# One gated mix of two attentions on one core: the phi of the segment tiles moved by a tile, its memory sums joined in pairs, weight loads and gates through GpSimd's queue

## The chip, the core and the metric

The kernel runs on one core of a Trainium2 chip. Five engines work in it, each through its own queue and strictly in the order in which the kernel was written: TensorE (PE, matrix products; PEld is its weight load), VectorE (DVE), ScalarE (ACT), GpSimd (POOL) and SyncE (SP), which here only starts DMA transfers. An engine that must wait for a semaphore holds up all that is queued behind the waiting instruction. The metric is device microseconds of one execution, smaller is better. The kernel before takes 1767.47 us, the median of three runs from 1766.33 to 1767.89 us.

## The reference, cut to what matters

```
x: [2048, 512]; 32 heads of 16
g = sigmoid(sum(x * gate_w))                        # per row
a = softmax(q k^T / 4) v @ A_wo                     # side A: plain attention, q k v = x @ wqkv
# side B: q, k, v = x @ wq, x @ wk, x @ wv, cut in 4 segments of 512 rows
phi(t) = t + 1 where t > 0, else exp(t)
g_h = sigmoid(beta)                                 # per head
M, z = 0, 0
for s in range(4):
    a_dot = causal softmax attention inside segment s
    a_mem = (phi(q_s) @ M) / (phi(q_s) @ z + 1e-6)
    o_s   = g_h * a_mem + (1 - g_h) * a_dot
    M += phi(k_s)^T @ v_s ;  z += sum over rows of phi(k_s)
b = o @ B_wo
out = g * a + (1 - g) * b
```

All is float32. phi is computed as max(t, 0) + exp(min(t, 0)).

## The kernel before, in words

**Two stages.** The first makes all projections and the memory M, z of side B; the second, from `wide` and `score_part` on, runs the attention itself, 32 units of side A and 32 of side B, and the output products. The change is all in the first stage.

**Slots.** The first stage is a row of slots. One slot is one projection tile: `slot()` (L350 to L363) issues twelve matmuls of 128x128 by 128x512 (L361), each factor split into a rounded value and its rest. After every third matmul comes a *place* (0 to 3) in which functions run that were posted for this slot with `post` (from here on) or `post_at` (a fixed slot). The list of a place runs in the order of posting. So the order of work on every engine is written out by hand, tile by tile.

**Side A first, then the segments.** Side A has 40 slots (chunks of 512 rows; the q tiles of the last two chunks are made later). Then come four segments of side B with twelve slots each: four q tiles (one per *octet* of eight heads), four v tiles, four k tiles. Below, slots are counted from the first segment's first q tile: segment c has q in 12c to 12c+3, v in 12c+4 to 12c+7, k in 12c+8 to 12c+11.

**What follows a q or k tile** is in `qk_tile` (L406). One slot after the matmuls run, in place 0, `e0`: ScalarE copies PSUM to `full` (L427), rounds it to `q1` (L428), SP stores that, and for tiles that need phi GpSimd takes `mn` = min(full, 0) (L432). In place 1, `e1`: VectorE makes the rest `q2` (L435), SP stores it, ScalarE takes `ex` = exp(mn) (L439). In place 2, `e2`: VectorE adds max(full, 0) to it (L444, `ph`). phi is needed for the k tiles of segments 0 to 2 and the q tiles of segments 1 to 3. `mn` and `ex` have one buffer each; `jk` of the gate (L525, VectorE) shares `mn`'s buffer.

**The memory.** For a k tile `mem_k` transposes phi on TensorE (L596, `tps`) at place 3 of the slot after the one in which `e2` ran, and ScalarE copies the result (`pt`, L598). After the second tile of a pair of octets `mem_k2` multiplies both by v (L610, `mps`, 64 small matmuls without the transposes), and `mem_k3` (L615) adds the sums to `mrun`, weighs them by the head's gate and a block mask into `mbd`, and spreads z into `zbd`: three small VectorE instructions for each octet, six for the pair (L618 or L620, L621, L622). `mem_q` (L564) reads all of it in slots 18, 30 and 42: `num` (L569, 32 matmuls) and `den` (L573) on TensorE.

**Maxima of the attention to come** are woven in. `some_max` runs at place 3 of slots 12 to 17 and 19 of a segment's round (and of all slots from 36 on but 42): four products (L236, `sm`) into four PSUM buffers, each read by one VectorE maximum (L269, `pm`). The next four products need these buffers back, and so does `num`. In segment 3, `load_gate` puts `jk` into slots 40 and 41.

**Weights and chunks** are loaded by `halves` (L375): two DMAs of 512 KB into `raw` tiles of which there are three, then a split by ScalarE (L397) and VectorE (L398) a few slots later. The three weights of the segments are loaded in this way during the last eight slots of side A, on SP's queue, where the stores of tiles are too (L424 for q and k, L470 for v). A load whose `raw` buffer is still being split waits at the head of its queue.

**Gates of the heads.** `betas` (L512) spreads 32 values of beta over the partitions with a matmul (L518) in slot 20 of side A, and takes the sigmoid.

Of the kernel before, what the change touches and what calls it, by code (L numbers as in the profile page):

```python
# [10 lines left out]
F32 = mybir.dt.float32  # L11
F32R = mybir.dt.float32r
AF = mybir.ActivationFunctionType
ALU = mybir.AluOpType
# [5 lines left out]
D = 512  # L20
# [27 lines left out]
def gated_mix(ctx, tc, x, xT, wqkv, a_wo, b_wq, b_wk, b_wv, b_wo, beta, gate_w, out):  # L48
# [278 lines left out]
    with ExitStack() as p0:  # L327
# [23 lines left out]
        def post(slots, place, f):  # L351
            posted.setdefault((now[0] + slots, place), []).append(f)
# [21 lines left out]

        def halves(pool, tag, src, load_slot, split_slot, tiles=None):  # L375

            hold = {}

            def load(i):
                t = tiles[i] if tiles else None  # L380
                if t is None:
                    t = raws.tile([128, 2, D], F32, tag="raw", name="raw")
                if isinstance(t, list):
                    for k in range(2):
                        nc.sync.dma_start(t[k], src[256 * i + 128 * k:256 * i + 128 * k + 128])
                        hold["raw", 2 * i + k] = t[k]
                else:
                    nc.sync.dma_start(t, src[256 * i:256 * i + 256].rearrange("(k p) d -> p k d", p=128))
                    for k in range(2):
                        hold["raw", 2 * i + k] = t[:, k]  # L390
# [21 lines left out]
        def qk_tile(side, w, xc, o, dst, then=None, ps=None, n0=0):  # L412
# [28 lines left out]
            def e2():  # L441
                if then:
                    ph["ph"] = wk.tile([128, CH], F32, tag="ph", name="ph", bufs=4)
                    nc.vector.scalar_tensor_tensor(ph["ph"], full, 0.0, ph["ex"], op0=ALU.max, op1=ALU.add)  # L444
                    then(ph["ph"])
            for place, f in enumerate((e0, e1, e2)):
                post(n0, place, f)

# [58 lines left out]
        gw = wk1.tile([128, D], F32, tag="gw", name="gw")  # L507
        beta8 = wk1.tile([8, NO], F32, name="beta8")
        post_at(8, 0, lambda: nc.gpsimd.dma_start(beta8, beta.rearrange("(o h) -> h o", h=8)))
        post_at(16, 0, lambda: nc.gpsimd.dma_start(gw, gate_w.unsqueeze(0).broadcast_to([128, D])))  # L510

        def betas():  # L512

            ps = me_ps.tile([128, CH], F32, tag="me", name="bt")
            spread = wk1.tile([8, 128], F32, name="spread")
            one8 = identf[0:8, 0:8]
            nc.vector.tensor_copy(spread.rearrange("p (h q) -> p h q", q=16), one8.unsqueeze(2).broadcast_to([8, 8, 16]))
            nc.tensor.matmul(ps[:, 0:NO], spread, beta8, start=True, stop=True)  # L518
            nc.scalar.activation(gh, ps[:, 0:NO], AF.Sigmoid)
            nc.vector.tensor_scalar(ogh, gh, -1.0, 1.0, op0=ALU.mult, op1=ALU.add)  # L520
        post_at(20, 2, betas)

        def gate_logit(xg, b, col):
            jk = wk1.tile([128, D], F32, tag="mn", name="jk")
            nc.vector.scalar_tensor_tensor(jk, xg[:, b], 1.0, gw, op0=ALU.mult, op1=ALU.mult,  # L525
                                           accum_out=glog[:, col:col + 1])
# [10 lines left out]
        for c in range(NCH):  # L537
            s0 = now[0] - (4 if c in LATER else 0)
            xn = halves(xp, "x", xchunk((c + 1) % NCH), s0 + (3 if c == 0 else 4), s0 + 8)
            if c == NCH - 1:  # L540
                wBq = halves(wp, "wq", b_wq, s0 + 7, s0 + 10)
                wBv = halves(wp, "wk", b_wv, s0 + 9, s0 + 13)
                wBk = halves(wp, "wv", b_wk, s0 + 11, s0 + 15)
            if c == 0:
                first_tiles(wAq, xc)
            for o in range(NO if 0 < c and c not in LATER else 0):
                qk_tile("A", wAq, xc, o, qd["A", o, c])
            for o in range(NO):
                qk_tile("A", wAk, xc, o, kd["A", o, c])
            v_tiles("A", wAv, xc, c)  # L550
            xc = xn

        mrun = [st.tile([128, 2, 17], F32, name=f"mrun{o}") for o in range(NO)]
        mbd = [st.tile([128, 2, DH], F32, name=f"mbd{o}") for o in range(NO)]
        zbd = st.tile([128, NO, 32], F32, name="zbd")
# [8 lines left out]
        def mem_q(c):  # L564

            banks = [me_sm.tile([128, CH], F32, tag="sm", name="num") for _ in range(4)]
            for o in range(NO):
                for i in range(4):
                    nc.tensor.matmul(banks[i][32 * o:32 * o + 32], mbd[o][32 * i:32 * i + 32].rearrange("p h e -> p (h e)"),  # L569
                                     pqs[o][32 * i:32 * i + 32], start=True, stop=True, tile_position=(32 * i, 32 * o))  # L570
# [34 lines left out]
        def mem_k2(both, c, vs):  # L605
            mps = me_ps.tile([128, 2, 2, 17], F32, tag="me", name="mps")
            for n, (o, pt) in enumerate(both):
                for b in range(4):
                    for i in range(4):
                        nc.tensor.matmul(mps[32 * i:32 * i + 32, n].rearrange("p h e -> p (h e)"), pt[:, b, 32 * i:32 * i + 32],  # L610
                                         vs[:, 2 * o + i // 2, b, 2 * (i % 2):2 * (i % 2) + 2].rearrange("p h e -> p (h e)"),
                                         start=(b == 0), stop=(b == 3), tile_position=(0, 32 * i))
            post(1, 0, lambda: mem_k3([o for o, _ in both], c, mps))

        def mem_k3(os, c, mps):  # L615
            for n, o in enumerate(os):
                if c == 0:
                    nc.vector.tensor_copy(mrun[o], mps[:, n])  # L618
                else:
                    nc.vector.tensor_add(mrun[o], mps[:, n], mrun[o])  # L620
                nc.vector.scalar_tensor_tensor(mbd[o], mrun[o][:, :, 0:16], gh[:, o:o + 1], bmask, op0=ALU.mult, op1=ALU.mult)  # L621
                nc.vector.tensor_scalar_mul(zbd[:, o, 0:8], heads8, mrun[o][:, 0, 16:17])  # L622

# [550 lines left out]
```

## Time and profile before

| | |
|---|---|
| median of three runs | 1767.47 us |
| the profiled execution's own time | 1768.02 us |
| its span in the trace | 1766.3 us |
| busy in the span: PE, DVE, ACT, POOL | 99%, 88%, 81%, 36% |
| first projection matmul (L455) | 5.91 us |
| `num` of segments 1, 2, 3 starts | 182.27, 230.20, 281.01 us |
| first scores of the second stage (L810) | 300.61 us |

Times in the trace count from the start of the span. A row of the timeline has the start, the length, engine, line, operation, output and inputs, and how many instructions are merged; in brackets stands the idle time of the engine ahead of it with what ended it. Instructions of one engine overlap at their ends, so what one costs in a dense row is the distance from its start to the next one's start. A row of the chain of waits has start, length, engine or queue, and line. A row of the windows has, for a stretch, each engine's busy time, then the granted TensorE clock (1.00 is full), the share of the DMA engines and GB/s.

### The profile page before, as it was taken

How to read it: one execution, taken by the hardware profiler on the slowest of the kernel's cores; microseconds unless marked ns; L12 is line 12 of the kernel's file. 1: busy time of each engine (PE TensorE's matmuls, PEld its weight loads, DVE VectorE, ACT ScalarE, POOL GpSimd, SP SyncE). 2: the span in 40 equal slices, each digit the busy share in tenths (PEclk: the TensorE clock that was granted, in tenths of full speed). 3: DMA queues.
4: the chain of work that ended last, by engine and by line, in shares of the span. 5: the costliest groups of instructions: out<-in, count | busy, mean ns of one | idle time of the engine just before them, and what ended most of it. 6: DMA issues, size and time to landing. Idle time of an engine off the chain costs nothing.

```text
span 1766.3 us, 41299 instructions
## 1 busy us (share of the span) xinstructions
PE 1755.0 (99%) x15231; PEld 901.0 (51%) x15231; DVE 1559.8 (88%) x3330; ACT 1435.2 (81%) x2751; POOL 642.5 (36%) x749
## 2 busy tenths in 40 slices
PE   9999999999999999999999999999999999999999
PEld 8886666544444444444444444444444444444444
DVE  4236667999999999999999999999999999999931
ACT  5454444888888898888888888888888888888884
POOL 3002222415161416443434343344434253434343
PEclk9999999999999999999999999999999999999999
DMA  7667665434453536554444545444545444544542
GB/s 244 219 227 224 201 219 185 124 111 135 125 157 108 148 109 177 147 142 134 132 141 123 147 128 147 129 145 110 155 115 151 127 137 120 151 120 143 150 154 62
DMA packets 149657, 261.60 MB, mean 148 GB/s; under 512 B 38568, under 2 KB 61128, under 8 KB 148944
## 3 DMA queue, kind: packets, MB, share of 16 engines
q1 hardware_dynamic: 148096, 257.56, 49.4%
q8 instruction: 121, 1.98, 0.5%
q0 software_dynamic: 1216, 1.14, 0.3%
q14 instruction: 80, 0.66, 0.1%
q10 hardware_dynamic: 144, 0.26, 0.1%
HBM read 174.39 MB, written 83.25 MB: 146 GB/s over the span
## 4 chain that ended last, share of the span: by engine, by line
PE 92%; DVE 3%; ACT 1%; POOL 1%; DMA 1%; issue 1%; SPq 0%; POOLq 0%; DVEq 0%; ACTq 0%
PE ops L155 40%; PE st L810 27%; PE sm L236 13%; PE pr L361 8%; PE sm L155 2%; DVE pm L269 2%; POOL mn L432 1%; DVE ph L444 1%; PE pr L455 1%; DMA qdB<-q 0%; DVE q L435 0%; DVE jk L525 0%; PE mt_ps L226 0%; ACT ex L439 0%; DMA raw<-xT 0%
## 5 line engine op out<-in xcount | busy, mean ns | idle before, releaser
L833 ACT ACTIVATE p<-st 128x512 f32<-128x512 f32 x2261 | 1190.7, 601 | 147.6 <-PE sm L236 92.1
L269 DVE TENSOR_REDUCE pm<-sm 128x1 f32<-128x512 f32 x2048 | 1276.7, 680 | 7.0 <-PE sm L236 7.0
L236 PE MATMUL sm<-kA,qA 48*128 48x512 f32 x2048 | 670.3, 425 | 3.8 <-DVE pm L269 2.1
L810 PE MATMUL st<-qA,kA 50*128 50x512 f32 x2014 | 656.0, 431 | 0.0
L155 PE MATMUL ops<-p,vA 128*17 128x256 f32 (+3 forms) x6360 | 552.6, 445 | 0.6 <-DMA qB<-mt 0.6
L810 PEld LDWEIGHTS st<-qA,kA 50*128 50x128 f32 x2014 | 326.8, 185 | 423.0 <-ACT p L833 382.7
L236 PEld LDWEIGHTS sm<-kA,qA 48*128 48x128 f32 x2048 | 340.5, 185 | 21.4 <-DVE pm L269 13.9
L934 POOL TENSOR_TENSOR rcp<-rec,minus 128x32 f32<-128x32 f32 x43 | 234.2, 5447 | 84.2 <-DMA rec<-dend 76.3
L284 DVE CUSTOM_DVE_ANT_0 rest<-sm,mask 128x128 f32<-128x128 f32 (+3 forms) x512 | 245.1, 479 | 0.7 <-PE sm L236 0.7
L155 PEld LDWEIGHTS ops<-p,vA 128*17 128x17 f32 x6360 | 129.3, 96 | 213.4 <-issue 182.3
L814 POOL TENSOR_SCALAR_AFFINE_SELECT p<-p 128x512 f32<-128x512 f32 x128 | 79.4, 636 | 289.9 <-ACT p L833 285.4
L236 PE MATMUL sm<-kB,qB 48*128 48x128 f32 (+3 forms) x512 | 166.0, 384 | 0.0
L810 PE MATMUL st<-qB,kB 50*128 50x512 f32 (+1 forms) x495 | 105.3, 329 | 0.3 <-ACT mt L229 0.3
L435 DVE TENSOR_TENSOR q<-full,q 128x512 fp32r<-128x512 f32 x56 | 38.6, 688 | 72.8 <-ACT q L428 66.3
L810 PEld LDWEIGHTS st<-qB,kB 50*128 50x128 f32 x495 | 68.5, 186 | 62.2 <-ACT p L833 50.5
L155 PE MATMUL ops<-p,vB 128*17 128x128 f32 (+3 forms) x1504 | 88.3, 350 | 0.0
L236 PEld LDWEIGHTS sm<-kB,qB 48*128 48x128 f32 x512 | 80.0, 184 | 0.0
L217 POOL CAST ms<-nm 128x16 fp32r<-128x16 f32 x32 | 6.3, 197 | 193.6 <-DVE nm L213 191.6
L432 POOL TENSOR_SCALAR mn<-full 128x512 f32<-128x512 f32 x24 | 37.8, 1576 | 96.9 <-ACT full L427 76.5
L427 ACT COPY full<-pr 128x512 f32<-128x512 f32 x56 | 32.7, 584 | 40.6 <-PE pr L361 34.5
L217 POOL CAST ms<-pm 128x16 fp32r<-128x16 f32 x32 | 6.3, 197 | 127.0 <-DVE pm L284 127.0
L950 POOL TENSOR_TENSOR v<-v,inv 128x512 f32<-128x512 f32 x31 | 39.8, 1285 | 27.4 <-DMA inv<-rdA 23.8
(197 smaller groups left out, 1578.9 us busy)
## 6 DMA issues: line engine op xcount, KB each, us to landing
kA<-kdA SPq DMA_DIRECT2D x256, 128.0 KB
vA<-vdA SPq DMA_DIRECT2D x31, 544.0 KB
kA<-kdA SPq DMA_DIRECT2D x256, 64.0 KB
qB<-qdB SPq DMA_DIRECT2D x192, 64.0 KB
kB<-kdB SPq DMA_DIRECT2D x192, 64.0 KB
kdA<-q SPq DMA_DIRECT2D x32, 256.0 KB
qdB<-q SPq DMA_DIRECT2D x32, 256.0 KB
qA<-qdA SPq DMA_DIRECT2D x64, 128.0 KB
```

Source lines behind the costliest of these rows:

```text
L155: behind[0] = nc.tensor.matmul(*args, **kw)
L236: nc.tensor.matmul(ps[:, n0:n0 + n], rows(qt[u][:, :, s * 128:(s + 1) * 128], h, 48), rows(k[:, :, k0:k0 + n], h, 48), start=True, stop=True)
L269: nc.vector.tensor_reduce(pm[:, h, s, kc:kc + 1], ps, axis=AX.X, op=ALU.max)
L284: nc.vector.tensor_tensor_reduce(out=tri["rest"][:, 0:w], in0=ps[:, n0:n0 + w], in1=tri["mask"][:, CH - w:], scale=-1.0, scalar=3.0e38, op ...
L361: nc.tensor.matmul(ps, l(a, k), r(b, k), start=(n == 0), stop=(n == 11))
L432: nc.gpsimd.tensor_scalar_min(ph["mn"], full, 0.0)
L435: nc.vector.tensor_sub(q2, full, q1.bitcast(F32))
L810: nc.tensor.matmul(ps[:, n0:n0 + CH - q0], rows(k[:, :, b * 128:(b + 1) * 128], h, 50), rows(q[:, :, q0:], h, 50), start=True, stop=True)
L814: nc.gpsimd.affine_select(out=x, in_=x, pattern=[[0, 4], [1, 128]], base=0, channel_multiplier=-1, compare_op=ALU.is_ge, fill=0.0)
L833: nc.scalar.activation(p[:, h], ps, AF.Exp, scale=SCALE)
L934: eng.tensor_tensor(r, rec, minus, op=ALU.pow)
L950: eng.tensor_mul(k["v"], k["v"], k["inv"])
```

## The change

Five edits:

1. **phi later.** `e2` is posted one slot later and in place 1 (it was place 2 of the slot of `e0` and `e1`). It runs there ahead of the next tile's `e1`. All that hangs on it (transposes, memory sums) moves by one slot; `mem_q` stays where it was.
2. **Memory sums for two octets at once.** `mrun` and `mbd` hold a pair of octets; `mem_k3` has three VectorE instructions for the pair. The gate and the block mask are multiplied ahead of time into `gmask`, in `betas`.
3. **Segment weights** are loaded from GpSimd's queue (three weights, two DMAs each).
4. **Gates of the heads** are spread by eight DMAs on GpSimd's queue in slot 8 of side A, straight into `gh`; the matmul, its operand and its PSUM tile are gone. `betas` has four more VectorE instructions.
5. **`jk`** uses the buffer of `dn` (`keep_den`) and not that of `mn`.

```diff
@@ -372,7 +372,7 @@
                 post_at(6 + i, 1 + 2 * r, lambda t=t, r=r: nc.gpsimd.dma_start(
                     raw(t)[64 * r + 48:64 * r + 50], ones.unsqueeze(1).broadcast_to([2, 2, CH])))
 
-        def halves(pool, tag, src, load_slot, split_slot, tiles=None):
+        def halves(pool, tag, src, load_slot, split_slot, tiles=None, queue=nc.sync):
 
             hold = {}
 
@@ -382,10 +382,10 @@
                     t = raws.tile([128, 2, D], F32, tag="raw", name="raw")
                 if isinstance(t, list):
                     for k in range(2):
-                        nc.sync.dma_start(t[k], src[256 * i + 128 * k:256 * i + 128 * k + 128])
+                        queue.dma_start(t[k], src[256 * i + 128 * k:256 * i + 128 * k + 128])
                         hold["raw", 2 * i + k] = t[k]
                 else:
-                    nc.sync.dma_start(t, src[256 * i:256 * i + 256].rearrange("(k p) d -> p k d", p=128))
+                    queue.dma_start(t, src[256 * i:256 * i + 256].rearrange("(k p) d -> p k d", p=128))
                     for k in range(2):
                         hold["raw", 2 * i + k] = t[:, k]
 
@@ -443,8 +443,9 @@
                     ph["ph"] = wk.tile([128, CH], F32, tag="ph", name="ph", bufs=4)
                     nc.vector.scalar_tensor_tensor(ph["ph"], full, 0.0, ph["ex"], op0=ALU.max, op1=ALU.add)
                     then(ph["ph"])
-            for place, f in enumerate((e0, e1, e2)):
-                post(n0, place, f)
+            post(n0, 0, e0)
+            post(n0, 1, e1)
+            post(n0 + 1, 1, e2)
 
         def first_tiles(w, xc):
 
@@ -505,23 +506,21 @@
         wAk = halves(wp, "wk", wqkv[:, D:2 * D], None, 2, [None, pairs[0]])
         wAv = halves(wp, "wv", wqkv[:, 2 * D:3 * D], 1, 4, [early[1].rearrange("p (k d) -> p k d", k=2), pairs[1]])
         gw = wk1.tile([128, D], F32, tag="gw", name="gw")
-        beta8 = wk1.tile([8, NO], F32, name="beta8")
-        post_at(8, 0, lambda: nc.gpsimd.dma_start(beta8, beta.rearrange("(o h) -> h o", h=8)))
+        gmask = wk1.tile([128, NO, 2, DH], F32, name="gmask")
+        for h in range(8):
+            post_at(8, 0, lambda h=h: nc.gpsimd.dma_start(gh[DH * h:DH * h + DH], beta.rearrange("(o h) -> h o", h=8)[h:h + 1]
+                                                          .broadcast_to([DH, NO])))
         post_at(16, 0, lambda: nc.gpsimd.dma_start(gw, gate_w.unsqueeze(0).broadcast_to([128, D])))
 
         def betas():
-
-            ps = me_ps.tile([128, CH], F32, tag="me", name="bt")
-            spread = wk1.tile([8, 128], F32, name="spread")
-            one8 = identf[0:8, 0:8]
-            nc.vector.tensor_copy(spread.rearrange("p (h q) -> p h q", q=16), one8.unsqueeze(2).broadcast_to([8, 8, 16]))
-            nc.tensor.matmul(ps[:, 0:NO], spread, beta8, start=True, stop=True)
-            nc.scalar.activation(gh, ps[:, 0:NO], AF.Sigmoid)
+            nc.scalar.activation(gh, gh, AF.Sigmoid)
             nc.vector.tensor_scalar(ogh, gh, -1.0, 1.0, op0=ALU.mult, op1=ALU.add)
+            for o in range(NO):
+                nc.vector.tensor_scalar_mul(gmask[:, o], bmask, gh[:, o:o + 1])
         post_at(20, 2, betas)
 
         def gate_logit(xg, b, col):
-            jk = wk1.tile([128, D], F32, tag="mn", name="jk")
+            jk = wk1.tile([128, D], F32, tag="dn", name="jk")
             nc.vector.scalar_tensor_tensor(jk, xg[:, b], 1.0, gw, op0=ALU.mult, op1=ALU.mult,
                                            accum_out=glog[:, col:col + 1])
 
@@ -538,9 +537,9 @@
             s0 = now[0] - (4 if c in LATER else 0)
             xn = halves(xp, "x", xchunk((c + 1) % NCH), s0 + (3 if c == 0 else 4), s0 + 8)
             if c == NCH - 1:
-                wBq = halves(wp, "wq", b_wq, s0 + 7, s0 + 10)
-                wBv = halves(wp, "wk", b_wv, s0 + 9, s0 + 13)
-                wBk = halves(wp, "wv", b_wk, s0 + 11, s0 + 15)
+                wBq = halves(wp, "wq", b_wq, s0 + 7, s0 + 10, queue=nc.gpsimd)
+                wBv = halves(wp, "wk", b_wv, s0 + 9, s0 + 13, queue=nc.gpsimd)
+                wBk = halves(wp, "wv", b_wk, s0 + 11, s0 + 15, queue=nc.gpsimd)
             if c == 0:
                 first_tiles(wAq, xc)
             for o in range(NO if 0 < c and c not in LATER else 0):
@@ -550,8 +549,8 @@
             v_tiles("A", wAv, xc, c)
             xc = xn
 
-        mrun = [st.tile([128, 2, 17], F32, name=f"mrun{o}") for o in range(NO)]
-        mbd = [st.tile([128, 2, DH], F32, name=f"mbd{o}") for o in range(NO)]
+        mrun = [st.tile([128, 2, 2, 17], F32, name=f"mrun{i}") for i in range(2)]
+        mbd = [st.tile([128, 2, 2, DH], F32, name=f"mbd{i}") for i in range(2)]
         zbd = st.tile([128, NO, 32], F32, name="zbd")
         nc.gpsimd.memset(zbd, 0.0)
 
@@ -566,7 +565,7 @@
             banks = [me_sm.tile([128, CH], F32, tag="sm", name="num") for _ in range(4)]
             for o in range(NO):
                 for i in range(4):
-                    nc.tensor.matmul(banks[i][32 * o:32 * o + 32], mbd[o][32 * i:32 * i + 32].rearrange("p h e -> p (h e)"),
+                    nc.tensor.matmul(banks[i][32 * o:32 * o + 32], mbd[o // 2][32 * i:32 * i + 32, o % 2].rearrange("p h e -> p (h e)"),
                                      pqs[o][32 * i:32 * i + 32], start=True, stop=True, tile_position=(32 * i, 32 * o))
             dps = me_ps.tile([128, CH], F32, tag="me", name="den")
             for o in range(NO):
@@ -610,16 +609,16 @@
                         nc.tensor.matmul(mps[32 * i:32 * i + 32, n].rearrange("p h e -> p (h e)"), pt[:, b, 32 * i:32 * i + 32],
                                          vs[:, 2 * o + i // 2, b, 2 * (i % 2):2 * (i % 2) + 2].rearrange("p h e -> p (h e)"),
                                          start=(b == 0), stop=(b == 3), tile_position=(0, 32 * i))
-            post(1, 0, lambda: mem_k3([o for o, _ in both], c, mps))
-
-        def mem_k3(os, c, mps):
-            for n, o in enumerate(os):
-                if c == 0:
-                    nc.vector.tensor_copy(mrun[o], mps[:, n])
-                else:
-                    nc.vector.tensor_add(mrun[o], mps[:, n], mrun[o])
-                nc.vector.scalar_tensor_tensor(mbd[o], mrun[o][:, :, 0:16], gh[:, o:o + 1], bmask, op0=ALU.mult, op1=ALU.mult)
-                nc.vector.tensor_scalar_mul(zbd[:, o, 0:8], heads8, mrun[o][:, 0, 16:17])
+            post(1, 0, lambda: mem_k3(both[0][0] // 2, c, mps))
+
+        def mem_k3(i, c, mps):
+            if c == 0:
+                nc.vector.tensor_copy(mrun[i], mps)
+            else:
+                nc.vector.tensor_add(mrun[i], mps, mrun[i])
+            nc.vector.tensor_mul(mbd[i], mrun[i][:, :, :, 0:DH], gmask[:, 2 * i:2 * i + 2])
+            nc.vector.tensor_mul(zbd[:, 2 * i:2 * i + 2, 0:8], heads8.unsqueeze(1).broadcast_to([128, 2, 8]),
+                                 mrun[i][:, :, 0, DH:DH + 1].broadcast_to([128, 2, 8]))
 
 
         def some_max():
```

## The prediction

> **What bounds the kernel now.** First the page.
>
> ```profile
> span 1766.3 us, 41299 instructions
> PE 1755.0 (99%) x15231; PEld 901.0 (51%) x15231; DVE 1559.8 (88%) x3330; ACT 1435.2 (81%) x2751; POOL 642.5 (36%) x749
> ...
> PE 92%; DVE 3%; ACT 1%; POOL 1%; DMA 1%; issue 1%; SPq 0%; POOLq 0%; DVEq 0%; ACTq 0%
> ```
>
> TensorE is the bound: 92% of the chain that ended last. No edit takes away TensorE work but one small matmul, so the change can win only where TensorE waits in the first stage: the 3% of DVE, and part of the ACT, POOL and DMA shares of the chain. A busy PE of 99% hides such waits, since the end of a matmul is modelled. So I read starts in TensorE's timeline. An undisturbed stretch comes first, then the rounds of the three segments.
>
> ```profile
> 293.38 0.73 PE L236 MATMUL sm<-kA,qA 48*128 48x512 f32 x4
> ...
> 296.99 0.73 PE L236 MATMUL sm<-kA,qA 48*128 48x512 f32 x4
> ```
>
> One slot with four max products lasts 296.99 - 293.38 = 3.61 us.
>
> ```profile
> 154.51 0.73 PE L236 MATMUL sm<-kA,qA 48*128 48x512 f32 x4
> 155.18 0.77 PE L610 MATMUL mps<-vs,pt 128*32 128x34 f32 x64
> 155.88 0.65 PE L596 MATMUL tps<-identf,ph 128*128 128x128 f32 x4
> 156.29 0.49 PE L361 MATMUL pr<-xh,wql 128*128 128x512 f32 x1
> ...
> 160.16 2.29 PE L236 MATMUL sm<-kA,qA 48*128 48x512 f32 x4 [0.84 <-DVE pm L269]
> ...
> 165.70 1.39 PE L236 MATMUL sm<-kA,qA 48*128 48x512 f32 x4
> ...
> 182.27 0.71 PE L569 MATMUL num<-ph,mbd 32*32 32x512 f32 x16
> ...
> 202.76 0.73 PE L236 MATMUL sm<-kA,qA 48*128 48x512 f32 x4
> ...
> 230.20 0.71 PE L569 MATMUL num<-ph,mbd 32*32 32x512 f32 x16
> ...
> 250.69 0.73 PE L236 MATMUL sm<-kA,qA 48*128 48x512 f32 x4
> ...
> 272.53 0.41 PE L226 MATMUL mt_ps<-identf,ms 128*32 128x128 f32 x2
> ...
> 281.01 1.14 PE L569 MATMUL num<-ph,mbd 32*32 32x512 f32 x32
> ```
>
> By distances of starts, `mps` costs 0.70 us and `tps` 0.41. From `sm` of the round's first slot (12) to `num` (slot 18) stand six slots, two `mps` and two `tps`: 6 x 3.61 + 2 x 0.70 + 2 x 0.41 = **23.88 us**, were nothing waited for. Found are 182.27 - 154.51 = 27.76, 230.20 - 202.76 = 27.44, and 281.01 - 250.69 = 30.32, of which `mt_ps` has a right to about 0.34. The excess is 3.88 + 3.56 + 6.10 = **13.54 us**. It sits where the reader sees `sm` of 2.29 and 1.39 us where 0.73 is normal: products that wait for maxima (L269) to give their PSUM back. In the third round there is more:
>
> ```profile
> 273.00:277.00 4.00, 4.00 (x11) 3.17 (x12) 3.96 (x9) 0.71 (x2) 0.00 (x0) 0.57 0.32 110
> ```
>
> The granted clock is 0.57 for these 4 us, right behind such a wait: 0.43 x 4 = 1.7 of the 6.10 us.
>
> Why are the maxima late? VectorE, GpSimd and ScalarE in the second round:
>
> ```profile
> 206.81 0.69 DVE L444 SCALAR_TENSOR_TENSOR ph<-full,ex 128x512 f32<-128x512 f32 x1 [2.04 <-ACT ex L439]
> 207.42 2.48 DVE L269 TENSOR_REDUCE pm<-sm 128x1 f32<-128x512 f32 x4
> 209.81 0.18 DVE L620 TENSOR_TENSOR mrun<-mps,mrun 128x34 f32<-128x34 f32 x1
> ...
> 210.85 0.69 DVE L435 TENSOR_TENSOR q<-full,q 128x512 fp32r<-128x512 f32 x1
> 211.46 0.68 DVE L444 SCALAR_TENSOR_TENSOR ph<-full,ex 128x512 f32<-128x512 f32 x1
> ```
>
> ```profile
> 204.35 1.77 POOL L432 TENSOR_SCALAR mn<-full 128x512 f32<-128x512 f32 x1 [3.40 <-DVE jk L525]
> ```
>
> ```profile
> 206.15 0.63 ACT L439 ACTIVATE ex<-mn 128x512 f32<-128x512 f32 x1 [2.92 <-POOL mn L432]
> ```
>
> `ph` stands ahead of the maxima in VectorE's queue and idles it for 2.04 us, waiting for `ex`, which waits for `mn`, which waited for `jk`, whose buffer it shares. So VectorE is late by waiting, not by work.
>
> **The change, part by part.** *phi later (edit 1) and `jk` apart (edit 5).* `ex` gets a whole slot more, and `mn` no longer waits for `jk`. What is late next? VectorE's own work. By starts: four maxima 209.81 - 207.42 = 2.39, the six small ones 210.85 - 209.81 = 1.04, `q2` 0.61, `ph` 207.42 - 206.81 = 0.61. Maxima begin about 0.54 after `sm`:
>
> ```profile
> 297.53 2.48 DVE L269 TENSOR_REDUCE pm<-sm 128x1 f32<-128x512 f32 x4 [0.38 <-PE sm L236]
> ```
>
> In the new order VectorE has, from one group of maxima to the next, 2.39 + `ph` 0.61 + `q2` 0.61 = 3.61 us, in slots 14 and 16 `mem_k3` besides, and in slot 17 no `q2`. TensorE's distances between the `sm` groups become 4.02 (slot 12, one `tps`), 4.72 (13, `mps` and `tps`), 4.02, 4.31, 3.61, 3.61. With `mem_k3` at half, 0.52, VectorE needs 3.61, 4.13, 3.61, 4.13, 3.00, and then 0.54 + 2.39 = 2.93 up to `num`. Each is below its distance; the least margin is 0.18 us. So rounds one and two lose their whole excess.
>
> Segment 3 has `jk` of its own in slots 40 and 41, of the same shape, 0.61 each: one falls between maxima 39 and 40, two between 40 and 41. With 0.12 for the row maximum of a finished unit (an estimate from the small ones) that is 4.13 + 0.73 = 4.86 against 4.31, late 0.55; then 2.39 + 3 x 0.61 = 4.22 against 3.61, late 1.16; `num` would start 0.54 + 1.16 + 2.39 = 4.09 after `sm` and not 3.61. **About 0.5 us of the wait stays there.** I take the slow clock as gone with the wait ahead of it.
>
> *Memory sums in pairs (edit 2).* Three instructions for six; over twice the columns they can't cost less than half, 0.52, and at worst 1.04 as now. At 1.04 slot 16's interval is 4.65 against 4.31, late 0.34, which the next two (3.00 of 3.61, 2.93 of 3.61) take up. So this edit is worth nothing on the path in rounds one and two, and up to 0.5 in round three.
>
> *Weights by GpSimd (edit 3).* The chain of waits before segment 0's first k tile:
>
> ```profile
> 121.06 0.56 DVE q L435
> ...
> 122.38 0.37 SPq L388
> ...
> 123.93 7.38 DMA qdB<-q
> ...
> 132.53 6.00 DMA raw<-xT
> ...
> 138.55 0.62 ACT xh L397
> ```
>
> ```profile
> 139.71 0.50 PE L361 MATMUL pr<-xh,wvl 128*128 128x512 f32 x1 [0.92 <-ACT vs L474]
> ```
>
> SP stands at the last weight load (L388) until its `raw` buffer is free at 122.38; the v store and the q stores are behind it. They crowd (7.38 us for one), VectorE waits for their buffers, and x, behind them all, is asked for at 132.53 and comes late: TensorE waits 0.92 us. With the weights in GpSimd's queue the first q stores go when `q2` is made, at 121.62, and not after 123.31 (the store that starts at 123.93 less its issue of about 0.6), and the v store ahead of them earlier still; so x comes some 1.7 us earlier, and 0.92 is enough. I take **0.92 us** gained; ends 0, if the transfers still crowd, and 1.1 with the slow first matmul behind the wait. GpSimd has only two memsets behind these loads, needed slots later. The price is in the load itself:
>
> ```profile
> 105.69 3.34 SPq L388 DMA_DIRECT2D raw<-b_wq  x2
> ```
>
> ```profile
> 112.84 0.62 ACT L397 CAST wqh<-raw 128x512 fp32r<-128x512 f32 x1 [2.92 <-DMA raw<-b_wq]
> 113.36 0.58 ACT L474 COPY vs<-pr 128x512 f32<-128x512 f32 x1
> ```
>
> ```profile
> vA<-vdA POOLq DMA_DIRECT2D x1, 544.0 KB, 4.2
> ```
>
> On SP `b_wq` takes 112.84 - 105.69 = 7.15 us behind other transfers; the one load of that size on GpSimd's queue landed in 4.2. The v copy behind it (113.36) frees PSUM for the next tile with about 0.25 us to spare, so each us of lateness beyond costs a us. I take the GpSimd load as no later than now: cost 0. A gain is excluded, since TensorE doesn't wait there now.
>
> *Gates by transfers (edit 4).* Eight small DMAs on an idle GpSimd, needed twelve slots later; four small VectorE instructions (a sixth of 1.04 us each, 0.7 in all), for which no tile waits: nothing, and 0.7 if that cover were gone. What goes is this:
>
> ```profile
> 63.37 0.39 PE L361 MATMUL pr<-wvh,xh 128*128 128x512 f32 x1
> ...
> 64.21 0.50 PE L361 MATMUL pr<-wvh,xl 128*128 128x512 f32 x1
> ```
>
> Between these two stands the matmul of `bt`: 64.21 - 63.37 less a tile's twelfth, 0.24 (2.94 / 12, the slot of 3.61 less its `sm` of 0.67), is **0.60 us** gained.
>
> *Sum.* 13.54 - 0.5 + 0.92 + 0.60 = 14.6 us. The profiled execution's own time is 1768.02 us: 1753.4. It lies 0.55 above the median of the runs, so the median should come to **1752.9 us**, 0.8% less. The second stage is TensorE's throughout and only shifts.
>
> **The Trainium skill against it.** GpSimd's `mn` is 1.77 above, and VectorE's `ph` beside an `mn` is 1.10 here, not 0.68:
>
> ```profile
> 219.70 1.10 DVE L444 SCALAR_TENSOR_TENSOR ph<-full,ex 128x512 f32<-128x512 f32 x1
> ```
>
> The Trainium skill (SBUF — State Buffer, section Who interferes with whom) says that a VectorE instruction with two SBUF inputs contends with a GpSimd instruction that reads SBUF; this row agrees. By that rule `ph` and `q2`, which will now lie beside `mn`, stretch it: rival B. The same page warns that descriptors of GpSimd's DMAs wait while VectorE runs copies in a two-port mode, but names `tensor_tensor` as free of it. VectorE's groups around the weight loads are all of that kind, as this one, so the warning doesn't bite here:
>
> ```profile
> L398 DVE TENSOR_TENSOR wql<-raw,wqh 128x512 fp32r<-128x512 f32 x4 | 2.7, 690 | 3.4 <-ACT wqh L397 3.4
> ```
>
> **The rivals.**
>
> *Clock (0.10): 1754.6.* The 3.4 us of half clock may come again elsewhere, as `num` and `den` keep TensorE thinly used: +1.7. For: one such stretch is there now. Against: two other waits of the same size had none. The Trainium skill (TensorE: Matmul & The Clock Gate, section What's actually happening) has a free-running window of 3.4 us for it, so that a drop is a matter of phase; one more can't be excluded by any row.
>
> *B, the wait moves to GpSimd (0.15): 1757, from 1755.5 to 1760.* If `mn` must wait for all of `ph` and `q2`, it takes 1.5 + 1.2 = 2.7 us, and ScalarE's loop `full`, `mn`, `ex`, `pt` 0.6 + 2.7 + 0.6 + 0.6 = 4.5 us against a mean slot of 23.88 / 6 = 3.98. Over six slots it falls 3.1 us behind; the added slot covers about 1.9; some 1.3 us wait is back in each of three rounds: +4.
>
> *C, weights late, but a gain (0.07): 1757 to 1763.* Loads 4 to 10 us later in all at slots 38 to 43 of side A.
>
> *It doesn't do what it says (0.07): 1764 to 1771.* The maxima stay late because VectorE's work, 3.61 of 3.61 us in most slots, needs more than these rows show (every `ph` and `q2` 0.4 longer makes 4.4 a slot, and the lag returns).
>
> *D, slower (0.06).* The three weights' loads in GpSimd's queue are starved. Place: the splits of side A's slots 38, 41 and 43, whose tiles follow at once. It decides where the three together come over 14.6 us later than their margins, some 5 us each, 12 us from issue to landing instead of 7.15; at 7 us each beyond them 1752.9 + 21 = 1774.
>
> **How the numbers follow.** 0.55 for the forecast (1751.5 to 1755.5), 0.10 clock, 0.15 B, 0.07 C, 0.07 no effect, 0.06 slower. The range 1751.5 to 1758.5 holds the first three, 0.8. A change of 0.2% (3.5 us) is about what a measurement of this kernel can tell from none: faster 0.55 + 0.10 + 0.15 + 0.07 = 0.87, same 0.07, slower 0.06.
>
> **What would show it.** Right: `sm` to `num` near 23.9 us in two rounds and near 24.5 in the third, no `sm` group of 1.3 us or more, no `[.. <-ACT ex]` ahead of `ph`, a clock of 1.00 at the third round, no gap at the first k tile, no `bt`. Wrong: `mn` of 2.5 us and `ph` waiting again (B); ScalarE waiting for `raw<-b_wq` longer than 2.92 us and TensorE for `vs` (C, D).

## The result, and the profile after

The changed kernel takes 1751.97 us, the median of 6 runs (1751.55 to 1753.31), against 1767.16 us for the kernel before (6 runs, 1766.22 to 1767.89): a ratio of 0.9916, with a 95% interval of 0.9904 to 0.9929. That is 15.2 us less; 14.6 had been forecast, and a time of 1752.9. Run again later on one chip beside the kernel before (e9 below), the change gave 14.2 us. Two executions far off all others, 1993.61 us of the kernel before beside e1 to e4 and 5827.38 us of e11, are left out of every median here. The profiled execution of the changed kernel took 1753.17 us, with a span of 1751.5.

The page of the changed kernel, engines and chain:

```profile
PE 1744.9 (100%) x15229; PEld 896.9 (51%) x15229; DVE 1560.8 (89%) x3315; ACT 1435.5 (82%) x2751; POOL 649.3 (37%) x762
...
PE 99%; DMA 0%; ACT 0%; issue 0%; POOL 0%; POOLq 0%; ACTq 0%
```

VectorE is as busy as it was (1560.8 us, 1559.8 before), and its 3% of the chain are gone: the same work, no longer waited for. The list of TensorE's waits says it too (us in total, times, longest). Two of its lines in the kernel before:

```profile
PE sm L236 <- DVE pm L269: 2.1, 3, 0.8
...
PE pr L361 <- ACT vs L474: 0.9, 1, 0.9
```

The whole list of the changed kernel:

```profile
PE idle L342 <- POOL heads L81: 1.4, 1, 1.4
PE ops L155 <- DMA qB<-mt: 0.8, 1, 0.8
PE st L809 <- ACT mt L229: 0.3, 1, 0.3
```

Both are gone. The 2.1 us are not the price of these waits, since a waiting matmul mostly shows as a long one; distances of starts give the price. TensorE's timeline of the changed kernel, the three rounds:

```profile
151.90 0.73 PE L236 MATMUL sm<-kA,qA 48*128 48x512 f32 x4
...
176.14 1.14 PE L568 MATMUL num<-ph,mbd 32*32 32x512 f32 x32
...
196.15 0.73 PE L236 MATMUL sm<-kA,qA 48*128 48x512 f32 x4
...
220.42 1.14 PE L568 MATMUL num<-ph,mbd 32*32 32x512 f32 x32
...
240.43 0.73 PE L236 MATMUL sm<-kA,qA 48*128 48x512 f32 x4
...
261.44 0.73 PE L236 MATMUL sm<-kA,qA 48*128 48x512 f32 x4
...
265.06 1.81 PE L568 MATMUL num<-ph,mbd 32*32 32x512 f32 x32
266.79 1.07 PE L572 MATMUL den<-ph,zbd 128*32 128x512 f32 x8
```

From `sm` of slot 12 to `num` the rounds now last 24.24, 24.27 and 24.63 us (27.76, 27.44 and 30.32 before). With phi a slot later one more `tps` (0.41) lies between these two marks, so without any wait they would last 23.88 + 0.41 = 24.29, and 24.63 in the third round with its `mt_ps`. **No wait is left ahead of `num`.** One is left at it: in the third round `num` lasts 266.79 - 265.06 = 1.73 to the start of `den`, where 1.07 is normal. VectorE of the changed kernel shows why:

```profile
261.98 0.69 DVE L524 SCALAR_TENSOR_TENSOR jk<-xg,gw 128x512 f32<-128x512 f32 x1
262.60 0.69 DVE L444 SCALAR_TENSOR_TENSOR ph<-full,ex 128x512 f32<-128x512 f32 x1
263.20 2.48 DVE L269 TENSOR_REDUCE pm<-sm 128x1 f32<-128x512 f32 x4
265.59 0.68 DVE L524 SCALAR_TENSOR_TENSOR jk<-xg,gw 128x512 f32<-128x512 f32 x1
```

The last maxima before `num` begin 263.20 - 261.44 = 1.76 after their `sm`, not 0.54: 1.22 late, behind a `jk` of segment 3's gates and a `ph`. VectorE goes on to the next instruction at 265.59, and the last of `num`'s four PSUM buffers comes free only about then.

The clock of the third round, in the windows of the changed kernel (after the busy times of the five engines stands the granted clock):

```profile
258.00:262.00 4.00, 4.00 (x20) 2.61 (x18) 3.97 (x9) 1.71 (x4) 0.00 (x0) 1.00 0.31 111
```

It is 1.00; the 0.57 of before is gone. Ahead of the rounds, TensorE of the changed kernel at the place of `bt` and at segment 0's first k tile:

```profile
63.38 0.39 PE L361 MATMUL pr<-wvh,xh 128*128 128x512 f32 x1
63.60 0.39 PE L361 MATMUL pr<-wvh,xl 128*128 128x512 f32 x1
...
137.50 0.39 PE L361 MATMUL pr<-wkh,xh 128*128 128x512 f32 x1
137.72 0.39 PE L361 MATMUL pr<-xh,wvl 128*128 128x512 f32 x1
```

Both tiles run through, 0.22 from matmul to matmul. Where the time came from, by starts: the first k tile comes 139.71 - 137.72 = 1.99 earlier, slot 12 of the first round 154.51 - 151.90 = 2.61, and the second stage 300.61 - 285.34 = 15.27. So 12.66 us lie between slot 12 and the second stage, and 1.99 ahead of the first k tile. The 0.62 between these two marks is mostly the `tps` that moved behind slot 12. The second stage takes about 0.5 us longer than before in these two traces (the spans differ by 14.8); why was not traced.

### The profile page after: what moved, and what is told of

It is laid out like the page before. It is cut to its first block, busy times and chain, and to the rows that moved or that the text cites. A ratio compares the mean times of both kernels' runs of the same rounds, so it can differ in the third digit from the quotient of the medians.

```text
span 1751.5 us, 41304 instructions
## 1 busy us (share of the span) xinstructions
PE 1744.9 (100%) x15229; PEld 896.9 (51%) x15229; DVE 1560.8 (89%) x3315; ACT 1435.5 (82%) x2751; POOL 649.3 (37%) x762
## 4 chain that ended last, share of the span: by engine, by line
PE 99%; DMA 0%; ACT 0%; issue 0%; POOL 0%; POOLq 0%; ACTq 0%
PE ops L155 40%; PE st L809 27%; PE sm L236 14%; PE pr L361 13%; PE sm L155 2%; PE pr L456 1%; PE mt_ps L226 0%; PE tps L595 0%; PE sm L809 0%; DMA qB<-mt 0%; PE idle L342 0%; PE mps L609 0%; PE num L568 0%; ACT p L832 0%; PE den L572 0%; PE ops L1115 0%
## 5 line engine op out<-in xcount | busy, mean ns | idle before, releaser
L236 PE MATMUL sm<-kA,qA 48*128 48x512 f32 x2048 | 662.7, 425 | 0.0
```

The lines of the kernel that those rows point to most:

```text
L236: nc.tensor.matmul(ps[:, n0:n0 + n], rows(qt[u][:, :, s * 128:(s + 1) * 128], h, 48), rows(k[:, :, k0:k0 + n], h, 48), start=True, stop=True)
```

## The experiments

The theory is the prediction's: TensorE waited because VectorE stood idle behind `ph`, edits 1 and 5 end that together, and the other gains are small ones of edits 3 and 4. Rivals: one of the two edits is enough; the rounds were late by VectorE's work, so that edit 2 counts; most of it is the clock; the first k tile needed the second queue, and not only a free head of SP's. The table has, for each kernel, what its three rounds take from `sm` of slot 12 to `num` over the same stretch without waits (23.88 us in the old order, 24.29 in the new one, 0.34 more in the third), then the time of `num` in the third round over 1.07, then the results. Medians are compared with runs of the kernel before on the same chip: 1766.07 us for e1 to e4, 1766.51 for e5 to e8, 1766.15 for e9 to e11.

| kernel | what it is | 1 | 2 | 3 | `num` | median | ratio, 95% interval |
|---|---|---|---|---|---|---|---|
| before | | 3.88 | 3.56 | 6.10 | 0 | 1767.16 | 1 |
| after | all five edits | 0 | 0 | 0 | 0.66 | 1751.97 | 0.9916 (0.9904 to 0.9929) |
| e1 | before + 1, 5 | 0 | 0 | 0.15 | 0.95 | 1753.23 | 0.9927 (0.9912 to 0.9942) |
| e2 | before + 5 | 1.01 | 0.80 | 3.31 | 0 | 1758.08 | 0.9955 (0.994 to 0.9969) |
| e3 | before + 3 | 4.26 | 3.59 | 6.09 | 0 | 1765.57 | 0.9998 (0.9988 to 1.0007) |
| e4 | after - 2 | 0 | 0 | 0.17 | 0.94 | 1752.05 | 0.9919 (0.9904 to 0.9934) |
| e5 | after - 1 | 0 | 0 | 2.38 | 0.36 | 1754.75 | 0.9933 (0.9916 to 0.9951) |
| e6 | before, loads later on SP | 3.82 | 3.58 | 4.73 | 0.38 | 1765.63 | 0.9997 (0.9987 to 1.0006) |
| e7 | after + VectorE work | 2.93 | 4.55 | 4.17 | 1.78 | 1765.58 | 0.9992 (0.9983 to 1.0002) |
| e8 | after, gates later | 0 | 0 | 0 | 0 | 1750.88 | 0.991 (0.9895 to 0.9926) |
| e9 | after again | 0 | 0 | 0 | 0.63 | 1751.95 | 0.9919 (0.9905 to 0.9933) |
| e10 | e8 again | 0 | 0 | 0 | 0 | 1751.46 | 0.9916 (0.9903 to 0.9929) |
| e11 | e8 - 1 | 0 | 0 | 3.71 | 0 | 1754.83 | 0.9937 (0.9921 to 0.9952) |

(Below 0.1 stands as 0; e7 lost another 0.96 at `num` of its first round.)

**e1: edits 1 and 5 alone.** The kernel before with

```diff
-            for place, f in enumerate((e0, e1, e2)):
-                post(n0, place, f)
+            post(n0, 0, e0)
+            post(n0, 1, e1)
+            post(n0 + 1, 1, e2)
-            jk = wk1.tile([128, D], F32, tag="mn", name="jk")
+            jk = wk1.tile([128, D], F32, tag="dn", name="jk")
```

> The kernel before with edits 1 and 5 alone (phi one slot later, jk in the buffer of dn); 1 can't stand without 5, since jk would take mn's buffer before ex has read it. Theory: VectorE was late by waiting for ex, not by work, so the three rounds lose their waits even with six small memory instructions a pair: sm to num 24.3 us in rounds one and two (23.88 and the one tps more that now lies inside), about 25.6 in the third (mt_ps 0.34 and about 1.0 of wait at num, since the six instructions cost 0.5 more there); time 1767.2 - 12.5 = 1754.7. The gap of 0.92 at the first k tile and bt stay. Rival, VectorE's work binds and the pairs are needed: 1 us or more of wait stays in each round, 1757.5 or more.

Measured: 1753.23 us. The first two rounds wait for nothing; the third keeps 0.15 ahead of `num` and 0.95 at it. TensorE of e1:

```profile
137.71 0.39 PE L361 MATMUL pr<-wkh,xh 128*128 128x512 f32 x1
138.15 0.50 PE L361 MATMUL pr<-xh,wvl 128*128 128x512 f32 x1
...
266.14 2.10 PE L570 MATMUL num<-ph,mbd 32*32 32x512 f32 x32
268.16 1.07 PE L574 MATMUL den<-ph,zbd 128*32 128x512 f32 x8
```

So these two edits carry 12.8 us here, where all five gave 15.2 and, run again, 14.2. One thing was not expected: the gap at the first k tile is 138.15 - 137.71 less a matmul's 0.22, only 0.22 us, though the weights load as before. That wait varies.

**e2: edit 5 alone**, the last two lines of that diff.

> The kernel before with edit 5 alone. Theory: mn starts some 2 us earlier in the two slots with jk, but ph still stands in its own slot ahead of the maxima and waits for ex; about half of the waits go: sm to num about 25.5 us in rounds one and two, time 1760 (1758 to 1762). Rival, the shared buffer was the whole cause: rounds near 23.9, time 1754 to 1755. Third possibility, nothing but moved waits: 1766 to 1768.

Measured: 1758.08 us, and 8.4 of the 13.5 us of excess gone. This is more than I gave it. TensorE of e2, the second round, and VectorE in it:

```profile
199.02 0.73 PE L236 MATMUL sm<-kA,qA 48*128 48x512 f32 x4
...
223.70 1.14 PE L569 MATMUL num<-ph,mbd 32*32 32x512 f32 x32
```

```profile
200.26 0.69 DVE L444 SCALAR_TENSOR_TENSOR ph<-full,ex 128x512 f32<-128x512 f32 x1 [1.03 <-ACT ex L439]
200.87 2.48 DVE L269 TENSOR_REDUCE pm<-sm 128x1 f32<-128x512 f32 x4
...
211.50 0.18 DVE L620 TENSOR_TENSOR mrun<-mps,mrun 128x34 f32<-128x34 f32 x1
...
212.54 0.68 DVE L435 TENSOR_TENSOR q<-full,q 128x512 fp32r<-128x512 f32 x1
213.14 1.10 DVE L444 SCALAR_TENSOR_TENSOR ph<-full,ex 128x512 f32<-128x512 f32 x1
```

The round takes 24.68 us where 23.88 would do. The first maxima of the round begin 200.87 - 199.02 = 1.85 after their `sm` (4.66 in the kernel before, 0.54 where nothing is late), mostly since the `ph` ahead of them still waits 1.03 for `ex`. VectorE doesn't make that up, because of the work behind it: the six small instructions (212.54 - 211.50 = 1.04), `q2`, and a `ph` of 1.10 beside a `mn`. So with `jk`'s buffer apart the long wait for `ex` of the first two rounds, 2.04 us, is down to half; the rest is the chain of `mn`, `ex` and `ph` itself, all in one slot. In the third round there is half clock again, 0.57 from 263 to 267 us.

**e3: edit 3 alone.** `queue=nc.gpsimd` for the three weights, as in the change.

> The kernel before with edit 3 alone. Theory: the gap of 0.92 us at the first k tile of the segments goes, and nothing else: 1766.2, rounds 27.8, 27.4 and about 30 us as before; the clock falls in the third round again if the wait ahead of it is the cause, unless the phase of its window decides. Rival, the x chunk is late by crowding of transfers whichever queue they are in: the gap stays, 1767.2.

Measured: 1765.57 us over 10 runs, 0.50 below its neighbours, which the interval can't tell from none. The first k tile has no gap. The rounds are those of before, the slow clock too, in the windows of e3:

```profile
271.00:275.00 4.00, 4.00 (x12) 3.00 (x11) 4.00 (x7) 0.73 (x2) 0.00 (x0) 0.57 0.28 92
```

**e4: all but edit 2.** The changed kernel with `mrun` and `mbd` for each octet and six small instructions:

```diff
-            nc.vector.tensor_mul(mbd[i], mrun[i][:, :, :, 0:DH], gmask[:, 2 * i:2 * i + 2])
+                nc.vector.scalar_tensor_tensor(mbd[o], mrun[o][:, :, 0:16], gh[:, o:o + 1], bmask, op0=ALU.mult, op1=ALU.mult)
```

> The changed kernel without edit 2 (six memory instructions a pair again, no gmask). Theory: rounds one and two stay at 24.3 us, the third gets about 0.5 us more wait at num than the changed kernel's 0.67; time 1752.0 + 0.5 = 1752.5. Rival, VectorE's work binds: waits of 0.5 us or more in each round, 1753.5 to 1757.

Measured: 1752.05 us. The third round keeps 0.17 + 0.94 = 1.11 us and not 0.66: with edit 1 in place, edit 2 is worth 0.45, in the third round alone, and nothing in the medians. e1 and e4 were run side by side and differ in edits 3 and 4: 1753.23 - 1752.05 = 1.18 us, where 1.52 had been forecast.

**e5: all but edit 1.**

```diff
-            post(n0, 0, e0)
-            post(n0, 1, e1)
-            post(n0 + 1, 1, e2)
+            for place, f in enumerate((e0, e1, e2)):
+                post(n0, place, f)
```

> The changed kernel without edit 1 (phi back in its own slot; edits 2 to 5 stay). Theory: what edit 5 alone leaves of the waits comes back, less about 0.5 us a round by the pairs: rounds one and two about 25 us, time 1757 (1755 to 1760). Rival, edit 1 is not needed once jk has its own buffer: 1752 to 1753.

Measured: 1754.75 us, a miss. TensorE of e5:

```profile
196.58 0.73 PE L236 MATMUL sm<-kA,qA 48*128 48x512 f32 x4
...
220.44 1.14 PE L567 MATMUL num<-ph,mbd 32*32 32x512 f32 x32
...
258.17 2.29 PE L236 MATMUL sm<-kA,qA 48*128 48x512 f32 x4 [0.52 <-DVE pm L269]
```

23.86 us: TensorE waits for nothing in the second round, nor in the first, without phi moved at all. VectorE still starts both late, behind a `ph` that waits 1.03 for `ex` as in e2, but with three small instructions for six it makes that up. Only in the third round does TensorE wait. GpSimd of e5 there, and VectorE:

```profile
253.73 0.20 POOL L217 CAST ms<-nm 128x16 fp32r<-128x16 f32 x1 [3.98 <-DVE nm L213]
...
254.20 1.92 POOL L432 TENSOR_SCALAR mn<-full 128x512 f32<-128x512 f32 x1
```

```profile
256.82 0.69 DVE L444 SCALAR_TENSOR_TENSOR ph<-full,ex 128x512 f32<-128x512 f32 x1 [2.04 <-ACT ex L439]
```

`mn` stands in GpSimd's queue behind `ms`, which waits for the finished row maximum `nm` of VectorE. So `ex` is late again and `ph` idles VectorE for 2.04 us, as long as it did behind `jk` before. Edit 1 covers this one place: 2.38 + 0.36 - 0.66 = 2.1 us of the third round, 2.8 by the medians.

**e6: the same loads on SP, the second halves asked for later.** The kernel before, its weights still in SP's queue:

```diff
-                post_at(load_slot, 3, lambda: load(1))
+                post_at(second or load_slot, 3, lambda: load(1))
-                wBq = halves(wp, "wq", b_wq, s0 + 7, s0 + 10)
-                wBv = halves(wp, "wk", b_wv, s0 + 9, s0 + 13)
-                wBk = halves(wp, "wv", b_wk, s0 + 11, s0 + 15)
+                wBq = halves(wp, "wq", b_wq, s0 + 7, s0 + 10, second=s0 + 8)
+                wBv = halves(wp, "wk", b_wv, s0 + 9, s0 + 13, second=s0 + 10)
+                wBk = halves(wp, "wv", b_wk, s0 + 11, s0 + 15, second=s0 + 13)
```

> The kernel before, weights on SP's queue as before, but the second half of each is asked for one or two slots later, when its buffer is free, so that SP doesn't stand in front of it. Theory (edit 3 helps since SP no longer stands ahead of the stores): the gap of 0.92 us at the first k tile goes without a second queue; 1766.2. Rival (it takes a second queue beside SP's to bring the weights and x in time): the gap stays or grows, 1767.2 or more.

Measured: 1765.63 us over 10 runs, 0.88 below its neighbours. TensorE of e6, first k tile and third round, and the two windows behind that wait:

```profile
138.85 0.39 PE L361 MATMUL pr<-wkh,xh 128*128 128x512 f32 x1
139.08 0.39 PE L361 MATMUL pr<-xh,wvl 128*128 128x512 f32 x1
...
269.50 2.28 PE L236 MATMUL sm<-kA,qA 48*128 48x512 f32 x4
```

```profile
269.00:273.00 4.00, 3.68 (x13) 1.74 (x12) 4.00 (x9) 1.62 (x4) 1.24 (x1) 1.00 0.18 66
273.00:277.00 4.00, 4.00 (x19) 2.75 (x18) 3.96 (x10) 0.59 (x1) 0.00 (x0) 1.00 0.42 134
```

The gap is gone without a second queue, and SP asks for x at 130.76 us, not at 132.53: what held up the v store, the q stores and x was a load that stood at the head of SP's queue before its buffer was free. And here the third round has its waits, up to an `sm` of 2.28 like the one ahead of the slow clock before, while the clock stays at 1.00.

**e7: more work on VectorE.** The changed kernel with two more instructions of 0.61 us in each of the slots 12 to 17 of the rounds; their result is not used:

```diff
+        def more():
+            for _ in range(2):
+                nc.vector.scalar_tensor_tensor(spare, gw, 1.0, gw, op0=ALU.mult, op1=ALU.mult)
+        for n in range(18):
+            post_at(now[0] + 12 * (1 + n // 6) + n % 6, 1, more)
```

> The changed kernel with two more VectorE instructions of 0.61 us (no use of their result) in each of slots 12 to 17 of the three rounds. Theory of the prediction's budget: VectorE then needs 4.83, 5.35, 4.83, 5.35, 4.22 and 2.93 us between groups of maxima, 27.5 in all against TensorE's 24.3: some 3 us wait in rounds one and two, 5 in the third: 1752 + 11 = 1763, sm groups of 1.3 us and more again. Rival, VectorE had slack beyond this sum: less than 3 us in all, under 1755.

Measured: 1765.58 us, 13.6 more than the changed kernel, somewhat above what was expected, with a stretch of half clock in it. So the prediction's budget, VectorE's time from maxima to maxima against TensorE's time from `sm` to `sm`, is the right yardstick: it is nearly full after the change, and of the 18 x 1.22 = 22 us put on it 13.6 come out at TensorE.

**e8, e9, e10: the last gates later.** The changed kernel with the `jk` of segment 3 out of slots 40 and 41:

```diff
-                post(4 + b // 2, 1 + 2 * (b % 2), lambda b=b: gate_logit(xg[b // 2], b % 2, 4 * c + b))
+                if c == NCH - 1:
+                    post(6 + b // 3, b % 3, lambda b=b: gate_logit(xg[b // 2], b % 2, 4 * c + b, "mn"))
+                else:
+                    post(4 + b // 2, 1 + 2 * (b % 2), lambda b=b: gate_logit(xg[b // 2], b % 2, 4 * c + b))
```

> The changed kernel with the four jk of segment 3 moved from slots 40 and 41 to slots 42 and 43 (slot 42 has no maxima), in mn's buffer, which is free by then. Theory: num of the third round is no longer late; it takes 1.07 us again and not 1.74, sm to num 24.6 us with mt_ps: 1752.0 - 0.7 = 1751.3. Rival, num waits for something else: 1.74 stays, 1752.0.

> The changed kernel once more, beside the two below on one chip. 1752.0; num of the third round 1.74 us again. How far its runs spread is read beside it: the ramp of the clock at the start moves the first chunk's end by up to 0.9 us between profiles.

> The changed kernel with segment 3's jk in slots 42 and 43, beside the changed kernel on one chip. Theory: 0.7 us less than it, by num alone: 1751.3. Rival, the difference seen in the first run (1750.9) was the ramp of the clock at the start: no difference between the two medians.

Measured: 1750.88 us, then 1751.46 beside 1751.95 for the changed kernel on the same chip. `num` of the third round in e10 is as long as in the first two rounds, 265.40 - 264.33 = 1.07 to `den`:

```profile
264.33 1.14 PE L571 MATMUL num<-ph,mbd 32*32 32x512 f32 x32
265.40 1.08 PE L575 MATMUL den<-ph,zbd 128*32 128x512 f32 x8
```

The last wait of the rounds, 0.66 us, was `jk`, as the prediction had it. The median moves by 0.5 us, less than the intervals can tell; e8 and e10 have the lowest medians here, ahead of the changed kernel by 0.5 to 1.1 us, of which the trace shows 0.66.

**e11: e10 without edit 1**, to see whether `jk` in slots 40 and 41 was what made phi's move necessary.

> As the kernel with jk in slots 42 and 43, but phi back in its own slot (edit 1 undone). Theory after the earlier runs: with jk's own buffer and pairs, edit 1 is worth only the third round's wait for GpSimd, where mn stands behind ms and ms waits for a row maximum; ph then idles VectorE 2.0 us there again. Without jk in slots 40 and 41 VectorE has 1.8 us less before num, so most of that is taken up: rounds one and two 23.9 us, third 24.2 to 25.5, time 1751 to 1753. Rival, edit 1 is needed in all rounds once anything moves: 1754 or more.

Measured: 1752.95, 1754.83 and 1757.2 us (the median is 1754.83). A miss: the third round keeps 3.71 us, half clock among it. VectorE of e11:

```profile
256.80 0.69 DVE L444 SCALAR_TENSOR_TENSOR ph<-full,ex 128x512 f32<-128x512 f32 x1 [2.04 <-ACT ex L439]
```

The 2.04 us are there with `jk` in slots 40 and 41 (e5) and without it, so they are those of `mn` behind `ms`: GpSimd of e11 again waits 3.98 us in `ms` for `nm` ahead of this `mn`. Edit 1 is needed in that round for them.

## Why the prediction was right, and where it was not

*The bound and the excess of 13.54 us: right.* The rounds last what six undisturbed slots last, to 0.05 us, and e7 brings the waits back by VectorE time alone. The mark "`sm` to `num` near 23.9" was wrong by its own change: it left out that a `tps` moves in between the two marks; 24.29 is the value without waits, and the distances of `sm` groups that it set against VectorE's work add up to it. One sign was not met: a wait of 0.42 us for `ex` stays ahead of `ph` in front of each round (at 149.67 in the first). VectorE has nothing else to do there, and TensorE doesn't wait.

*"phi later (edit 1) and `jk` apart (edit 5)": the step that was not right, though its sum was.* It took the two together and said that VectorE's work then fits. The experiments part them. Edit 5 alone takes 8.4 of 13.5 us (e2). What is left in the first two rounds is a wait of 1.03 us and too much work behind it to make it up. Edit 1 ends the wait (e1, without pairs), edit 2 shortens the work (e5, without phi later), and with either TensorE waits for nothing there. Only in the third round is edit 1 needed (e5, e11). I had read the wait for `ex` as one mechanism. Besides the chain's own length it has two causes, `mn` behind `jk` in all rounds and `mn` behind `ms` in the third, and the second stood in the trace of before, in the third round on GpSimd:

```profile
266.26 0.20 POOL L217 CAST ms<-nm 128x16 fp32r<-128x16 f32 x1 [4.54 <-DVE nm L213]
...
266.78 1.49 POOL L432 TENSOR_SCALAR mn<-full 128x512 f32<-128x512 f32 x1
```

This `mn` has no bracket of its own, since the engine waited in the instruction ahead of it; looking for brackets at `mn` misses it. In the kernel before it cost `ph` only 0.80 us of waiting, since VectorE was late by then; with `jk` out of the way it is the 2.04 of e5.

*"Worth nothing on the path in rounds one and two, up to 0.5 in round three" (edit 2): right beside edit 1* (0.45 by e4), and not a property of the edit: from e2 to e5 the first two rounds gain 1.8 us, and the two kernels differ there in edit 2 alone, edits 3 and 4 acting ahead of the rounds. The price of the three instructions was sized at half or all of 1.04 us. VectorE of the changed kernel, first round:

```profile
154.84 0.81 DVE L444 SCALAR_TENSOR_TENSOR ph<-full,ex 128x512 f32<-128x512 f32 x1
...
158.82 0.21 DVE L616 COPY mrun<-mps 128x68 f32<-128x68 f32 x1
...
159.22 0.60 DVE L620 TENSOR_TENSOR zbd<-heads,mrun 128x16 f32<-128x16 f32 x1
159.74 0.68 DVE L444 SCALAR_TENSOR_TENSOR ph<-full,ex 128x512 f32<-128x512 f32 x1
```

From the copy to `ph` they take 159.74 - 158.82 = 0.92 us here, with a `zbd` of 0.60 beside a `mn` of GpSimd; after the second pair 0.49 (167.54 to 168.03).

*The sum: close in part by luck.* The first k tile comes 1.99 us earlier and not 0.92 + 0.60 = 1.52, and the second stage, said only to shift, takes 0.5 more; the two nearly cancel.

*"About 0.5 us of the wait stays there": right in place and cause* (`jk`, e10), 0.66 in size. The working was 1.16 late; 1.22 is measured.

*Weights by GpSimd, 0.92: right in mechanism, loose in size.* x is asked for earlier, by SP of the changed kernel at

```profile
130.32 0.93 SPq L388 DMA_DIRECT2D raw<-xT  x2
```

and not at 132.53, and TensorE no longer waits. e6 shows that the head of SP's queue was the cause. But the wait of 0.92, and 1.08 by starts, was that of one execution: with the same loads it is 0.22 in e1 and 0.33 in e2. None of the ten traces with the loads moved has any, so the wait goes, but its worth isn't a fixed number. Alone the edit gives 0.50 (e3), too little to be told from none. *Gates by transfers, 0.60:* the gap at `bt` went, 0.84 to 0.22 by starts. The two edits together give 1.18 by the medians of e1 and e4, 1.52 in the sum. A further 0.3 us between these two places I have not traced.

*The rivals.* The clock did not drop again, and e2, e3 and e11 show that it could have. Its price of 1.7 us was too high as a share of the third round: e6, at full clock, loses 4.73 + 0.38 = 5.11 us there and the kernel before 6.10, about 1.0 more. B asked whether `mn` would stretch beside `ph` and `q2`, by the rule of the Trainium skill (SBUF — State Buffer, section Who interferes with whom) that the two contend. GpSimd of the changed kernel, beside the first `ph` above:

```profile
154.49 1.49 POOL L432 TENSOR_SCALAR mn<-full 128x512 f32<-128x512 f32 x1 [2.25 <-ACT full L427]
```

They do contend, but here VectorE pays: `mn` keeps its 1.49, `ph` takes 0.81 for 0.68. It starts 0.35 after `mn` and ends before it, so neither waits for the whole of the other. That costs 0.13 us of VectorE's slack where I had put 1.2 on ScalarE's loop. Where a `ph` starts first, ahead of the round (146.94 us), the `mn` behind it (147.24) takes 1.73. C and D, weights late: on GpSimd's queue of the changed kernel the first load goes at

```profile
88.70 0.74 POOL L388 DMA_DIRECT2D raw<-b_wq  x1 [9.40 <-DMA kdA<-q]
```

17 us earlier than on SP (105.69): GpSimd had reached it by then, and its buffer was free. The second half goes at 108.14, about when it did on SP (108.64). ScalarE waited 2.92 for the first half before; in the changed kernel it waits only for the second:

```profile
112.99 0.62 ACT L397 CAST wqh<-raw 128x512 fp32r<-128x512 f32 x1 [1.16 <-DMA raw<-b_wq]
```

## What to carry to other kernels

Where an engine with little slack idles in front of one instruction, follow that instruction's inputs through every queue they pass, one round at a time: the same wait can have different causes in different rounds, and here the buffer shared between two engines was removed by one word and was worth 8 of the 15 us. Two edits that each give the same engine slack needn't add up; take each away alone before either is called needed or useless. A transfer posted before its buffer is free holds up all that is behind it in that queue: here it was enough to post it later (e6), and also to put it into another queue (e3).

## What the runs showed of the hardware

**The same long wait came with the slow clock and without it.** Four microseconds at a granted clock of 0.57 or 0.58 came in the third round of before, e2, e3 and e11 and in the second of e7, each beginning within some 3.5 us of the start of an `sm` of about 2.3 us; e6 has such an `sm` in the same round, and e5 too, and both stay at 1.00. No kernel without such an `sm` in its rounds had the slow clock. That would fit the free-running window that the Trainium skill (TensorE: Matmul & The Clock Gate, section What's actually happening) describes. What tips it, no run here shows.

**The same kernel's traces start differently.** Slot 12 of the first round comes at 151.90 us in the traces of after and e9, at 151.18 in e10, with the same instructions up to there. The difference arises in the first four projection matmuls, which take 7.63 - 5.81 = 1.82 us by starts in after and 6.90 - 5.89 = 1.01 in e10. A difference of half a microsecond between two kernels must therefore be read between two marks of one trace, not from its start.
